# New states in 64x64 tiles over two PSUM banks, ahead of the values from the state, in an mLSTM with an MLP behind it

## The chip, the cores and the metric

One core of a Trainium2 chip runs the whole kernel. The metric is the time of one execution on the device, in microseconds (us); lower is better. All engines of the core (TensorE, VectorE, ScalarE, GpSimd, and SyncE, which issues most DMAs) work on the one program and wait for each other by semaphores.

## What is computed

An mLSTM over 4 batches, 8 heads, 768 steps of time and heads of width 40, followed by a gated MLP (320 to 2048 to 320) on all 3072 tokens, in float32:

```python
for t in range(S):
    m_new = np.maximum(f_gate[:, :, t] + m, i_gate[:, :, t])
    f_stab = np.exp(f_gate[:, :, t] + m - m_new)
    i_stab = np.exp(i_gate[:, :, t] - m_new)
    m = m_new
    C = f_stab[:, :, None, None] * C + i_stab[:, :, None, None] * np.einsum('bhd,bhe->bhde', vt, kt)
    n = f_stab[:, :, None] * n + i_stab[:, :, None] * kt
    h_tilde = np.einsum('bhde,bhe->bhd', C, qt)
    denom = np.maximum(np.abs(np.einsum('bhd,bhd->bh', n, qt)[:, :, None]), 1.0)
    y[:, :, t] = 1.0 / (1.0 + np.exp(-o_gate[:, :, t])) * h_tilde / denom
...
h = x @ w_in
return (h * (1.0 / (1.0 + np.exp(-h))) @ w_out).astype(np.float32)
```

## The kernel before, in words

Time is cut into 12 chunks of 64 steps, the batches into 2 pairs. A *unit* is one chunk of one pair: 64 steps x 2 batches x 8 heads; there are 24, numbered 0 to 23. Three units make a *step* of 384 tokens for the MLP (8 steps, `j`), and the MLP of a step walks over 16 blocks of 128 hidden features (`fc`).

For a unit, `scores` (L516) multiplies keys and queries of the chunk, `weigh` (L550, instruction at L551) multiplies the scores by the decay in place, `near_values` (L587, matmuls at L595) applies them to the values of the chunk, `far_values` (L604, L610) adds what comes from the state Cm of the chunks before, `norm`, `level` and `scale` (L619 to L655) divide by the denominator and apply the output gate, which gives x. `state` (L660) makes what the chunk adds to the state (pu, from the weighted keys kw and the values vt), and `carry` (L677) decays the state on GpSimd (L688) and adds pu to it on VectorE (L694), for the two halves `a` of the partitions in turn. Chunk 11 has no new state, so units 0 to 21 have one. Scores and near values run in 64x64 tiles of TensorE; far values and states use all rows (104 or 128) and 64 columns. The values are 41 wide, as a column of ones brings the denominator along.

From step 2 on, x is turned by a transposition on VectorE (`turn_out`, L701), four writes to DRAM (L703) and, two `fc` later, a read back (`turn_in`, L711), all on SyncE's queue; five `fc` after the block ScalarE and VectorE split it into a high and a low part (`xput`, L740 and L741). In steps 0 and 1 TensorE transposes x (L729).

The MLP of step j and the units of step j + 1 are woven together by hand: the schedule is manual, and the order of the program is the order on each engine. `mm1` (L761, matmuls at L784) makes ph for one `fc`, 8 matmuls from step 1 on; `act` (L788) makes the tanh on ScalarE (L791), then the gating on VectorE (L805, L797 in step 0), the high part on ScalarE (L810), the low part on VectorE (L814); `mm2` (L819, matmuls at L835) uses them two `fc` later. Three places in each step (PLACES, L41: `fc` 1, 5 and 9 from step 2 on) hold a unit's block. There TensorE gets, between `mm1` and `mm2`,

```python
        if n + 1 < NU:
            units[n + 1].scores(pair)
        u.place(pair)
        u.near_values()
        u.far_values()
        u.state()
```

so the scores of the next unit and the values of this one lie in one PSUM tile (`couple`, psP, one buffer). The weighting of unit n + 1 and the norm of unit n follow in `close` (L879), from within `act`, and level, scale, turn_out and carry behind it. ph lies in the pool psH, two banks used in turn; pu lies in psU, one bank. A tile can be written once every access to the tile that had its buffer before is done.

Of the kernel before, what the change touches and what calls it, by code (L numbers as in the profile page):

```python
# [8 lines left out]
F32 = mybir.dt.float32  # L9
# [5 lines left out]
ALU = mybir.AluOpType  # L15
# [3 lines left out]
B, H, S, D = 4, 8, 768, 40  # L19
L = 64  # L20
# [6 lines left out]
UPS = 3  # L27
# [3 lines left out]
D1 = D + 1  # L31
# [12 lines left out]
def mlstm_mlp_kernel(  # L44
# [12 lines left out]
    nc = tc.nc  # L57
# [7 lines left out]
    psH = pool("psH", 2, space=PSUM)  # L65
    psP = pool("psP", 1, space=PSUM)
    psU = pool("psU", 1, space=PSUM)
# [12 lines left out]
    for k in range(2):  # L80
        m = mask[k * L : (k + 1) * L]
        nc.gpsimd.affine_select(
            out=m, in_=m, compare_op=ALU.is_ge, fill=NEG, base=0,
# [264 lines left out]
    def bank(n, pool_, tag, shape, name):  # L348

        if n < UPS:  # L350
            return pool_.tile(shape, F32, tag=tag, name=name)
        return psU.tile(shape, F32, tag="u", name=name)

    def couple(name):

        return psP.tile([128, H, 128], F32, tag="p", name=name)

    class Unit:
# [301 lines left out]
        def state(self):  # L660
            n, c, p = self.n, self.c, self.p
            if c == NC - 1:
                return
            pu = bank(n, psO, "o", [128, H, D1], f"pu{n}")
            by_d = pu.rearrange("p (d j) f -> p j d f", d=2)
            for j in range(4):
                for a in range(2):
                    nc.tensor.matmul(  # L668
                        by_d[a * 64 : a * 64 + D, j],
                        self.kw[:, a * 4 + j, :],  # L670
                        self.vt[:, :, a * 4 + j, :],
                        start=True,
                        stop=True,
                    )
            self.pu = pu

        def carry(self, copy=nc.scalar.copy):  # L677
            n, c, p = self.n, self.c, self.p
            if c == NC - 1:
                return  # L680
            pu = self.pu
            for a in range(2):
                r = slice(a * 64, a * 64 + D)
                v = Cm[p][r, a, :].rearrange("p (h e) -> p h e", e=D1)
                if c == 0:
                    copy(v, pu[r])
                    continue
                nc.gpsimd.tensor_tensor(  # L688
                    out=v,
                    in0=v,  # L690
                    in1=self.lq[r, :, L - 1].unsqueeze(2).broadcast_to([D, H, D1]),
                    op=ALU.mult,
                )
                nc.vector.tensor_tensor(out=v, in0=v, in1=pu[r], op=ALU.add)  # L694

        def turn_out(self):

# [168 lines left out]
    def block(n):  # L866

        u = units[n]
        if n + 1 < EARLY and n + 2 < NU:
            units[n + 2].load()  # L870
        pair = couple(f"p{n + 1}")
        if n + 1 < NU:
            units[n + 1].scores(pair)
        u.place(pair)
        u.near_values()
        u.far_values()
        u.state()

    def close(n):  # L879
        if n + 1 < NU:  # L880
            units[n + 1].weigh()
        units[n].norm()

    def turn(n):
        if n + 1 >= EARLY and n + 3 < NU:
            units[n + 3].load()
        if n + 2 < NU:
            units[n + 2].load_q()
            units[n + 2].shift()
        if n % UPS == 0:  # L890
            steps[n // UPS] = Step(n // UPS)
        if n < 3 * UPS:
            units[n].xpose()
            units[n].xput(steps[n // UPS])
# [172 lines left out]
    for j in range(NSTEP):  # L1067
        st = steps[j]
        for fc in range(NFC):
            at = {}  # L1070
            if j < NSTEP - 1:
                at = {fc - a: units[(j + 1) * UPS + u] for u, a in enumerate(PLACES[min(j, 2)])}
            if j == 0 and fc in KEYS:
                units[KEYS[fc]].keys()
            st.mm1(fc)
            if 0 in at:
                block(at[0].n)
                st.act(fc, between=lambda: close(at[0].n))
                at[0].level()
                at[0].scale()  # L1080
                if j > 1:
                    at[0].turn_out()
                at[0].carry()
            else:
                st.act(fc, splits=[SPLITS[x[0]](int(x[1])) for x in LOWS.get((j, fc), ())])
            if 2 in at and at[2].n + 1 < NU:
                if at[2].n + 2 < NU:
                    units[at[2].n + 2].exp()
                units[at[2].n + 1].misc()
            if j > 0 and 3 in at and at[3].n + 2 < NU:  # L1090
                units[at[3].n + 2].keys()
            if fc >= LAG and (j, fc) != (NSTEP - 1, NFC - 1):
                st.mm2(fc - LAG)
            elif fc < LAG and j > 0:
                steps[j - 1].mm2(NFC - LAG + fc)
            if 1 in at:
                turn(at[1].n)
                if at[1].n + 2 < NU:
                    units[at[1].n + 2].add()
            if j > 1 and 5 in at:  # L1100
                at[5].xput(steps[j + 1])
            if j > 1 and 2 in at:
                at[2].turn_in()
            if j == 0:
                FILL[fc]()
# [78 lines left out]
```

## Time and profile before

| | us |
|---|---|
| median of 3 runs | 441.98 |
| lowest and highest | 441.46, 442.47 |
| the profiled execution's own time | 440.74 |
| its span, first to last instruction | 439.0 |
| TensorE busy | 433.2 (99%) |
| VectorE busy | 278.0 (63%) |
| ScalarE busy | 211.8 (48%) |
| GpSimd busy | 124.2 (28%) |

The granted clock of TensorE is full in all 40 slices of the profile. Names in the rows: PE is TensorE's matmuls, PEld its weight loads, which overlap them, DVE is VectorE, ACT ScalarE, POOL GpSimd, SP SyncE. L595 is line 595 of the kernel. `p<-vb,D` reads: tile p is written from vb and D. Where a row of the timeline merges instructions of one line, the second number is the time from the start of the first to the end of the last.

### The profile page before, as it was taken

How to read it: one execution, taken by the hardware profiler on the slowest of the kernel's cores; microseconds unless marked ns; L12 is line 12 of the kernel's file. 1: busy time of each engine (PE TensorE's matmuls, PEld its weight loads, DVE VectorE, ACT ScalarE, POOL GpSimd, SP SyncE). 2: the span in 40 equal slices, each digit the busy share in tenths (PEclk: the TensorE clock that was granted, in tenths of full speed). 3: DMA queues.
4: the chain of work that ended last, by engine and by line, in shares of the span. 5: the costliest groups of instructions: out<-in, count | busy, mean ns of one | idle time of the engine just before them, and what ended most of it. 6: DMA issues, size and time to landing. Idle time of an engine off the chain costs nothing.

```text
span 439.0 us, 11120 instructions
## 1 busy us (share of the span) xinstructions
PE 433.2 (99%) x4437; PEld 399.9 (91%) x4437; DVE 278.0 (63%) x610; ACT 211.8 (48%) x439; POOL 124.2 (28%) x135
## 2 busy tenths in 40 slices
PE   8999999999999999999999999999999999999996
PEld 4767667799999999999999999999999999999995
DVE  5798789577875577466664676455674655444442
ACT  7783955545744444444444533544344444443332
POOL 5834144133233243134230444122341311000000
PEclk9999999999999999999999999999999999999999
DMA  8999796251350565406751265603854131101001
GB/s 265 368 367 321 198 285 161 83 171 44 116 142 1 128 181 143 129 16 189 200 147 31 57 195 157 173 2 90 243 119 128 18 90 37 36 2 45 1 1 46
DMA packets 58644, 56.29 MB, mean 128 GB/s; under 512 B 28208, under 2 KB 45184, under 8 KB 58592
## 3 DMA queue, kind: packets, MB, share of 16 engines
q1 hardware_dynamic: 58288, 55.15, 44.0%
q8 instruction: 35, 0.57, 0.6%
q10 hardware_dynamic: 208, 0.26, 0.2%
q0 software_dynamic: 96, 0.16, 0.1%
q14 instruction: 17, 0.14, 0.1%
HBM read 48.59 MB, written 6.96 MB: 127 GB/s over the span
## 4 chain that ended last, share of the span: by engine, by line
PE 80%; issue 16%; DVE 1%; DMA 1%; ACT 1%; POOL 0%; POOLq 0%; DVEq 0%; ACTq 0%
PE ph L784 35%; PE pout L835 32%; PE p L524 3%; PE p L610 3%; PE pu L668 3%; PE p L595 2%; DMA home<-in_ig_dram 1%; PE p L729 0%; PE po L579 0%; PE px L729 0%; DVE D L551 0%; POOL qt L508 0%; PE pt L198 0%; PE ph L913 0%; PE e L384 0%
## 5 line engine op out<-in xcount | busy, mean ns | idle before, releaser
L791 ACT ACTIVATE th<-ph 128x384 f32<-128x384 f32 x128 | 62.5, 488 | 128.1 <-PE ph L784 127.6
L784 PE MATMUL ph<-xh,wh 128*128 128x384 f32 x336 | 113.9, 339 | 0.0
L784 PE MATMUL ph<-xl,wh 128*128 128x384 f32 x336 | 113.7, 338 | 0.0
L805 DVE SCALAR_TENSOR_TENSOR th<-th,ph 128x384 f32<-128x384 f32 x112 | 62.1, 555 | 74.2 <-ACT th L791 73.5
L835 PE MATMUL pout<-woh,gh 128*128 128x320 f32 x336 | 105.4, 314 | 0.0
L835 PE MATMUL pout<-woh,gl 128*128 128x320 f32 x336 | 103.9, 309 | 0.0
L835 PE MATMUL pout<-wol,gh 128*128 128x320 f32 x336 | 103.2, 307 | 0.0
L814 DVE TENSOR_TENSOR gl<-th,gh 128x384 fp32r<-128x384 f32 x112 | 65.5, 585 | 47.6 <-ACT gh L810 47.6
L810 ACT CAST gh<-th 128x384 fp32r<-128x384 f32 x112 | 57.5, 513 | 71.8 <-DVE th L805 71.2
L784 PE MATMUL ph<-xh,wl 128*128 128x384 f32 x224 | 76.0, 339 | 0.0
L835 PEld LDWEIGHTS pout<-woh,gh 128*128 128x128 f32 x336 | 63.0, 188 | 2.0
L784 PEld LDWEIGHTS ph<-xh,wh 128*128 128x128 f32 x336 | 63.1, 188 | 0.2
L835 PEld LDWEIGHTS pout<-woh,gl 128*128 128x128 f32 x336 | 63.0, 188 | 0.1
L784 PEld LDWEIGHTS ph<-xl,wh 128*128 128x128 f32 x336 | 63.0, 188 | 0.2
L835 PEld LDWEIGHTS pout<-wol,gh 128*128 128x128 f32 x336 | 63.1, 188 | 0.0
L688 POOL TENSOR_TENSOR Cm<-Cm,lq 40x328 f32<-40x328 f32 x40 | 30.5, 763 | 110.2 <-PE p L610 108.6
L508 POOL TENSOR_TENSOR qt<-qk,lq 104x512 f32<-104x512 f32 x22 | 28.7, 1306 | 115.6 <-ACT lq L504 103.0
L784 PEld LDWEIGHTS ph<-xh,wl 128*128 128x128 f32 x224 | 42.1, 188 | 0.0
L835 PE MATMUL pout<-wo,g 128*128 128x320 f32 x96 | 28.7, 435 | 0.0
L491 POOL TENSOR_TENSOR D<-D,am 128x512 f32<-128x512 f32 x20 | 26.2, 1310 | 5.9 <-DMA D<-LFd 3.9
L483 POOL TENSOR_TENSOR am<-mask,aT 128x512 f32<-128x512 f32 x20 | 24.1, 1206 | 6.6 <-DVE aT L205 5.1
L551 DVE TENSOR_TENSOR D<-p,D 128x512 f32<-128x512 f32 x24 | 16.5, 689 | 11.7 <-PE p L610 10.3
(126 smaller groups left out, 490.2 us busy)
## 6 DMA issues: line engine op xcount, KB each, us to landing
qk<-in_qk_dram SPq DMA_DIRECT2D x24, 512.0 KB, 4.9
ko<-in_ko_dram SPq DMA_DIRECT2D x24, 320.0 KB, 5.1
wro<-in_w_out_dram SPq DMA_DIRECT2D x8, 640.0 KB, 6.8
D<-LFd SPq DMA_DIRECT2D x40, 128.0 KB, 3.1
lq<-LFd SPq DMA_DIRECT2D x40, 128.0 KB, 4.5
wri<-in_w_in_dram SPq DMA_DIRECT2D x8, 512.0 KB, 5.8
vb<-in_vp_dram SPq DMA_DIRECT2D x48, 82.0 KB, 4.5
out_dram<-ob SPq DMA_DIRECT2D x45, 80.0 KB, 2.1
```

The costliest lines, as they stand in the source:

```text
L483: nc.gpsimd.tensor_tensor(out=self.am, in0=mask.unsqueeze(1).broadcast_to([128, H, L]), in1=aT[:, self.c, self.p, :].unsqueeze(2).broadcas ...
L491: nc.gpsimd.tensor_tensor(out=self.Dm, in0=self.Dm, in1=self.am, op=ALU.add)
L508: nc.gpsimd.tensor_tensor(out=self.qt, in0=self.q[:KS], in1=self.lq[:KS], op=ALU.mult)
L524: nc.tensor.matmul(self.ps[d * L : (d + 1) * L, a * 4 + j, :], self.k[r, d * 4 + j, :], self.q[r, d * 4 + j, :], start=True, stop=True,)
L551: nc.vector.tensor_tensor(out=self.Dm, in0=self.ps, in1=self.Dm, op=ALU.mult)
L688: nc.gpsimd.tensor_tensor(out=v, in0=v, in1=self.lq[r, :, L - 1].unsqueeze(2).broadcast_to([D, H, D1]), op=ALU.mult,)
L784: nc.tensor.matmul(ph, w, x, start=(i == 0), stop=(i == len(ops) - 1))
L791: nc.scalar.activation(th, ph, AF.Tanh, scale=0.5)
L805: nc.vector.scalar_tensor_tensor(out=th, in0=th, scalar=1.0, in1=ph, op0=ALU.add, op1=ALU.mult)
L810: nc.scalar.copy(gh, th)
L814: nc.vector.tensor_tensor(out=gl, in0=th, in1=gh.bitcast(F32), op=ALU.subtract)
L835: nc.tensor.matmul(self.po[t], g[:, ts], w, start=(fc == 0 and i == 0), stop=(last and i == len(ops) - 1),)
```

## The change

For units from the fourth on (`n >= UPS`, UPS is 3), the new state is made in 64x64 tiles: the two batches of the pair (d, which lie on the two halves of the partitions) are no longer one matmul over 128 rows and 82 columns (the other batch's values are zero in each half), but two over 64 rows and 41 columns. The part of d = 0 goes to a bank of psU, that of d = 1 to a bank of psH. The new state comes ahead of the far values. `carry` adds the parts one by one, four additions of 40x164 for two of 40x328, and it stands ahead of `turn_out`.

```diff
@@ state
+            if n >= UPS:
+                self.pu = [
+                    pool_.tile([128, 4, D1], F32, tag=tag, name=f"pu{n}_{tag}")
+                    for pool_, tag in ((psU, "u"), (psH, "h"))
+                ]
+                for j in range(4):
+                    for d in range(2):
+                        r = slice(d * L, (d + 1) * L)
+                        for a in range(2):
+                            nc.tensor.matmul(
+                                self.pu[d][a * 64 : a * 64 + D, j, :],
+                                self.kw[r, a * 4 + j, :],
+                                self.vt[r, d, a * 4 + j, :],
+                                start=True,
+                                stop=True,
+                            )
+                return
@@ carry
-                nc.vector.tensor_tensor(out=v, in0=v, in1=pu[r], op=ALU.add)
+                for d in range(2) if n >= UPS else ():
+                    w = v[:, d * 4 : (d + 1) * 4]
+                    nc.vector.tensor_tensor(out=w, in0=w, in1=pu[d][r], op=ALU.add)
+                if n < UPS:
+                    nc.vector.tensor_tensor(out=v, in0=v, in1=pu[r], op=ALU.add)
@@ block
         u.near_values()
+        u.state()
         u.far_values()
-        u.state()
@@ the loop over steps and fc
                 at[0].level()
                 at[0].scale()
+                at[0].carry()
                 if j > 1:
                     at[0].turn_out()
-                at[0].carry()
```

## Rows read from the trace of the kernel before

**Rows 1.** The page, busy us, share of the span and instructions of each engine.
```profile
PE 433.2 (99%) x4437; PEld 399.9 (91%) x4437; DVE 278.0 (63%) x610; ACT 211.8 (48%) x439; POOL 124.2 (28%) x135
```
**Rows 2.** Waits: who waited for whom: us in total, times, longest us.
```profile
DVE D L551 <- PE p L610: 10.3, 16, 0.7
...
ACT xh L740 <- DMA px<-xd: 2.9, 4, 1.3
```
**Rows 3.** Timeline of TensorE around unit 13: start, length in us, instructions.
```profile
203.08 0.63 PE L595 MATMUL p<-vb,D 64*64 64x41 f32 x32
203.64 0.79 PE L610 MATMUL p<-Cm,qt 104*64 104x82 f32 x16
204.25 0.74 PE L668 MATMUL pu<-vb,kw 128*40 128x82 f32 x16
204.92 0.42 PE L835 MATMUL pout<-woh,gh 128*128 128x320 f32 x1
205.18 0.31 PE L835 MATMUL pout<-wol,gh 128*128 128x320 f32 x1
205.32 0.31 PE L835 MATMUL pout<-woh,gl 128*128 128x320 f32 x1
...
206.34 0.34 PE L784 MATMUL ph<-xh,wh 128*128 128x384 f32 x1
...
209.05 0.34 PE L784 MATMUL ph<-xh,wh 128*128 128x384 f32 x1
```
**Rows 4.** Timeline of TensorE, windows that end at 203.19 and 203.25.
```profile
203.08 0.34 PE L595 MATMUL p<-vb,D 64*64 64x41 f32 x12
...
203.08 0.40 PE L595 MATMUL p<-vb,D 64*64 64x41 f32 x16
```
**Rows 5.** Single lines, weight loads and matmuls: ns min/median/max, first and last start.
```profile
L784 PEld LDWEIGHTS ph<-xh,wh x336: 186/188/190, 80.7 to 430.2; 128*128 128x128 f32 x168
...
L595 PEld LDWEIGHTS p<-vb,D x672: 129/135/135, 36.7 to 369.7; 64*64 64x64 f32 x168
...
L668 PEld LDWEIGHTS pu<-vb,kw x352: 112/115/118, 12.7 to 345.0; 128*40 128x40 f32 x176
L668 PE MATMUL pu<-vb,kw x352: 232/233/267, 12.7 to 345.1; 128*40 128x82 f32 x176
```
**Rows 6.** Timeline of VectorE around unit 13.
```profile
203.53 0.56 DVE L805 SCALAR_TENSOR_TENSOR th<-th,ph 128x384 f32<-128x384 f32 x1 [0.72 <-ACT th L791]
...
206.93 0.68 DVE L655 SCALAR_TENSOR_TENSOR x<-ko,p 128x256 f32<-128x256 f32 x3
207.65 0.58 DVE L701 STREAM_TRANSPOSE xt<-x 128x384 f32<-128x384 f32 x1
208.15 0.98 DVE L694 TENSOR_TENSOR Cm<-Cm,pu 40x328 f32<-40x328 f32 x2
```
**Rows 7.** VectorE's groups by shape: busy us, mean ns, idle us before.
```profile
L694 DVE TENSOR_TENSOR Cm<-Cm,pu 40x328 f32<-40x328 f32 x40 | 19.2, 479 | 0.7
L655 DVE SCALAR_TENSOR_TENSOR x<-ko,p 128x256 f32<-128x256 f32 x21 | 8.9, 422 | 0.7
...
L655 DVE SCALAR_TENSOR_TENSOR x<-ko,p 128x64 f32<-128x64 f32 x42 | 7.3, 214 | 0.0
```
**Rows 8.** Timeline, VectorE and weight loads, behind unit 3 in step 0.
```profile
46.62 0.69 DVE L257 SCALAR_TENSOR_TENSOR wi<-wri 128x512 uint32<-128x512 uint32 x1 [0.52 <-ACT wri L256]
...
47.36 0.62 PEld L784 LDWEIGHTS ph<-x,wi 128*128 128x128 f32 x3 [0.52 <-DVE wi L257]
```
**Rows 9.** Timeline of VectorE and TensorE behind unit 6, in step 1.
```profile
93.25 1.01 DVE L694 TENSOR_TENSOR Cm<-Cm,pu 40x328 f32<-40x328 f32 x2
...
95.04 0.43 PE L784 MATMUL ph<-xh,wh 128*128 128x384 f32 x1
```
**Rows 10.** Timeline, the turned x of unit 14 and the next step's first matmul.
```profile
235.30 0.56 DVE L741 TENSOR_TENSOR xl<-px,xh 128x384 fp32r<-128x384 f32 x1 [0.74 <-ACT xh L740]
...
236.13 0.34 PE L784 MATMUL ph<-xh,wh 128*128 128x384 f32 x1
```

## The prediction, made before the change had run

> **What bounds the kernel now.** I read the busy shares first. TensorE is busy 433.2 of 439.0 us [rows 1], and in the middle of the run nothing stops it, so time is gained only where TensorE's own stream gets shorter, and any new wait in that stream is paid in full. The view of waits, read second, names TensorE in no long wait; it shows two queues hanging on it that matter here. VectorE's weighting (L551) waits 16 times for the end of the far values (L610), although what it needs is the scores: scores and values share one PSUM tile. And ScalarE already waits four times for the turned x to come back from DRAM [rows 2].
>
> Third, the timeline of one block, unit 13 in step 3; the others from unit 9 on look alike within 0.03 us. The near values start at 203.08, the far ones at 203.64, the state at 204.25, and MLP work goes on at 204.92 [rows 3]. The first matmul of the next fc comes at 206.34 and that of the one after it at 209.05 [rows 3]. 19 units (3 to 21) have the changed state: three in step 0, three in step 1, thirteen later.
>
> **The state on TensorE.** Each fp32 matmul is two records. Today's state is 16 records in pairs; they last 0.74 with 0.233 for the last [rows 3, 5], so the eight pairs are 0.072 apart, 0.57 in all. The new one is 32 records in eight groups of four, in the tile form of the near values, with 41 moving columns and 40 weight columns for 64. What is a group worth? The near values give the upper end: between 12 and 16 records the stretch grows from 0.34 to 0.40 [rows 4], so 0.058 a group (0.06 as shown; 32 records fit in 0.56). The lower end is half of today's pair, since half the columns pass: 0.036. Which one holds depends on what sets the near values' pace. A weight load takes 188 ns for 128 columns, 135 for 64, 115 for 40 [rows 5]: 0.83 ns a column, 53 ns for 64, just under the 58, and 33 for 40. I read the 58 as the load's pace, and then 40 columns run at the matmul's own; I take 0.040, nearer the lower end. The state then pushes the far values back by 0.058 + 7 x 0.040 = 0.34 (0.31 to 0.46), and TensorE gains 0.57 - 0.34 = 0.23 a block (0.11 to 0.26). Leaving the 64x64 form costs a pause either way: it stands before the far values today and will stand there again. That MLP work follows the far values instead of the state I cost at nothing, as both fill all rows in 64 columns (bound: 0.1 either way).
>
> If all of that came through, 19 x 0.23 = 4.4 us would go. Two things stand against it.
>
> **The borrowed bank.** Half the state now takes a place in the ring of two banks that hold ph. The next ph (206.34) must therefore wait for this fc's L805, done at 204.09 [rows 3, 6]: a margin of 2 us, so nothing. But the ph after that (209.05) takes the bank in which the state lies, and waits until VectorE's last addition has read it. VectorE's chain runs from the far values' end without a gap: weighting, norm, gl, level, scale, ending at 206.93 + 0.68 = 207.61 [rows 6]. It moves with the far values, by 0.34. Then come four additions of 164 elements for two of 328. One of 328 takes 479 ns; L655 takes 422 ns for 256 elements and 214 for 64, or 1.08 ns an element [rows 7], so 164 take about 0.31. Three L655 in a row last 0.68 where their own times add up to 0.85: instructions on the same partitions overlap by 0.085. Today's two additions, on different partitions, last 0.98 [rows 6] and don't overlap. The new order is two on one partition range, then two on the other: 4 x 0.31 - 2 x 0.085 + 0.03 = 1.10 (0.98, as today, if half the length costs half; 1.33 if nothing overlaps). They may start 0.08 before the scale ends, as today's start at 208.15 before the transposition ends at 208.23 [rows 6]. So the bank is free at 207.61 - 0.08 + 0.34 + 1.10 = 208.97, and 0.05 later the weight load can start, as it did behind L257 (ends 47.31, load at 47.36) [rows 8]. A matmul behind a cold load loses another 0.11: 204.92 to 205.18 is 0.26, the next step 0.15 [rows 3]. That gives 209.13. Without the wait it would be 209.05 - 0.23 = 208.82. So the block gains 0.23 and then waits 0.31: **0.08 lost**, and 0.05 in the five first blocks of a step, which start 0.02 later: 8 x 0.08 + 5 x 0.05 = 0.89 us.
>
> In steps 0 and 1 the transposes of x lie in between and there is no turning through DRAM. In step 1 the additions start at 93.25 [rows 9]: 93.25 + 0.34 + 1.10 + 0.05 + 0.11 = 94.85 against 95.04 today; 0.19 gained, three times, 0.57. In step 0 there is more room, but after unit 3 TensorE waits 0.52 for a weight part anyway [rows 8], which eats that unit's share: 2 x 0.23 = 0.46.
>
> **The addition ahead of turn_out.** The transposition (L701, 207.65 [rows 6]) now starts behind the additions, at 209.00: 1.35 later. Behind it on SP's queue stand the four writes to DRAM, the output's stores in a step's first block, the next unit's loads, and the read of the turned x; they follow each other almost without gaps, so all move. The loads are issued some three blocks ahead and stay covered; the read is less so. Of the four waits for it [rows 2] one is a step's third unit, 14: its xl is done at 235.30 + 0.56 = 235.86, and the next step's first matmul is at 236.13 [rows 10]. With 1.35 more, that matmul waits about 1.1. The other three waits are of first units, whose late x delays only an activation. I take 0.5 (0 to 2). That L805 of the next fc stands behind additions and transposition (0.45 later) costs nothing: its bank is wanted 1.5 us later.
>
> **Sum.** 0.89 - 0.57 - 0.46 + 0.5 = +0.4 us. On the profiled execution (440.74 us, 439.0 span) that is 441.1; against the median of 441.98, 1.2 above it, **442.3 us**, no change. A measurement of this kernel tells some 0.2% (0.9 us) from nothing. This case by itself spans 441.0 to 444.0.
>
> **Rivals.**
> *The state runs at the near values' pace* (0.058). For it: it is the only four-tile row with 41 columns. Against it: the load's length per column. The far values then move 0.46 and the block gains only 0.11; the ph waits until 209.25: 8 x 0.20 + 5 x 0.17 = 2.45 lost, 0.2 and 0.2 gained in steps 1 and 0, 0.5 for x: 444.5. It decides from 0.05 a group on.
> The Trainium skill (TensorEngine Tiling (Array Packing), Instruction Overhead) gives each matmul some 60 cycles of overhead, so that one of 1 column takes as long as one of 60; by that rule the 41 columns set the near values' pace, not the weights, the state would get the same 0.058, and the time would be this rival's rather than the sum's. The weight rows of this case speak for the other reading, without excluding it.
> *The bank comes back later still*: the four additions don't overlap (1.33), or the four tiles take turns in twos, so that the change doesn't do what it says. Either adds 0.23 to each wait: 13 x 0.3 = 3.9, with 0.5 for x and little gained before: 446. For it: today's additions don't overlap. Against it: L655 does.
> *The bank comes back in time*: faster. It would need VectorE to be done 0.35 earlier, with shorter additions or a weighting that no longer waits for the far values; then each block keeps its 0.23 and the time goes down to 437.6, or to some 440 if half of the wait goes. For it: four terms of the chain are estimates of a tenth each. Against it: the 16 waits of L551.
>
> **Chances.** The forecast 0.42 (same 0.31, slower 0.09, faster 0.02); near values' pace 0.18, slower; later still 0.15, slower but for 0.02; in time 0.25, of it 0.02 within 0.2%. That makes faster 0.25, same 0.35, slower 0.40. The range leaves a tenth out on each side: 439.6 to 445.8.
>
> **What would show it.** The state's records in groups of four some 0.04 apart (0.058 for the rival) and the far values 0.34 behind today's place; a wait of ph (L784) for the additions to Cm, 13 times, some 0.3 each, two fc after each block from step 2 on, and none in step 0; the four additions within 1.1; ScalarE's wait for px grown by about 1.3 each. No wait of L784 for VectorE would make the prediction wrong on the fast side; waits of 0.5 on the slow side.

## The result, and the profile after

| us | before | after |
|---|---|---|
| median, same chip (6 runs each) | 441.49 | 444.70 |
| lowest and highest | 441.3, 442.47 | 443.2, 445.76 |
| the profiled execution's own time | 440.74 | 444.32 |
| its span | 439.0 | 442.5 |

The change makes the kernel slower, by 0.7%: ratio 1.0067 [1.0046, 1.0087], 3.2 us. The range (439.6 to 445.8) held the time, but the forecast, no change, did not come: 442.3 was 2.4 us too low. Of the change itself, +0.4 forecast, 2.8 were missing, as the kernel before is 0.5 faster here than the median that the prediction started from.

The page's first and fourth part, of the kernel after:
```profile
span 442.5 us, 11784 instructions
...
PE 432.1 (98%) x4741; PEld 395.3 (89%) x4741; DVE 282.2 (64%) x648; ACT 211.2 (48%) x439; POOL 123.1 (28%) x135
...
PE 60%; issue 18%; DVE 12%; DMA 5%; ACT 3%; SPq 2%; POOL 0%; POOLq 0%; DVEq 0%; ACTq 0%
```
TensorE is busy 1.1 us less than before [rows 1] in a span that is 3.5 longer: its stream did get shorter, and it now stands still at times. The last line is the chain of work that ended last, followed back from the end. Before, it ran through VectorE and DMAs for 1% each; now 12% and 5%. The view of waits says where:
```profile
DVE D L551 <- PE p L610: 13.8, 16, 1.0
ACT xh L761 <- DMA px<-xd: 7.1, 7, 1.9
...
PEld ph L805 <- PE pout L856: 5.0, 12, 0.4
...
PE ph L805 <- DVE Cm L713: 3.5, 13, 1.3
```
Each line gives us in total, times, and the longest. The last is new: ph (now L805) waits 13 times for the additions to Cm (L713). The line above it is the weight load of the same ph, which stands just ahead of the matmul and whose wait the profile puts down to pout; the two overlap, so their totals aren't added. ScalarE's wait for the turned x went from four times and 2.9 us [rows 2] to seven times and 7.1.

The timeline of TensorE around unit 13 (its near values start at 203.83, against 203.08 before):
```profile
203.83 0.63 PE L595 MATMUL p<-vb,D 64*64 64x41 f32 x32
204.27 0.21 PE L673 MATMUL pu_u<-vb,kw 64*40 64x41 f32 x1
...
204.31 0.20 PE L673 MATMUL pu_u<-vb,kw 64*40 64x41 f32 x1
...
204.55 0.20 PE L673 MATMUL pu_u<-vb,kw 64*40 64x41 f32 x1
...
204.70 0.79 PE L610 MATMUL p<-Cm,qt 104*64 104x82 f32 x16
205.41 0.42 PE L856 MATMUL pout<-woh,gh 128*128 128x320 f32 x1
...
206.83 0.34 PE L805 MATMUL ph<-xh,wh 128*128 128x384 f32 x1
...
209.89 0.41 PE L805 MATMUL ph<-xh,wh 128*128 128x384 f32 x1 [0.19 <-DVE Cm L713]
210.14 0.34 PE L805 MATMUL ph<-xl,wh 128*128 128x384 f32 x1
```
```profile
209.86 0.19 PEld L805 LDWEIGHTS ph<-xh,wh 128*128 128x128 f32 x1 [0.42 <-PE pout L856]
```
The first record of the first group of four tiles is at 204.27, of the second at 204.31, of the eighth at 204.55: 0.040 a group. The far values come 0.87 behind the near ones (0.56 before [rows 3]), the first mm2 1.58 (1.84 before), the next fc's ph 3.00 (3.26 before). So TensorE's stream is 0.26 shorter. The ph after that comes at 6.06 behind the near values, against 5.97 before [rows 3], and its second matmul is 0.25 later, not 0.17 as in a warm stream: the 0.26 is gone, and more.

VectorE's timeline of the same block, and the additions' groups by shape (busy us, mean ns, idle us before):
```profile
205.53 0.69 DVE L551 TENSOR_TENSOR D<-p,D 128x512 f32<-128x512 f32 x1 [0.70 <-PE p L610]
...
207.99 0.68 DVE L655 SCALAR_TENSOR_TENSOR x<-ko,p 128x256 f32<-128x256 f32 x3
208.59 0.31 DVE L713 TENSOR_TENSOR Cm<-Cm,pu_u 40x164 f32<-40x164 f32 x1
208.83 0.31 DVE L713 TENSOR_TENSOR Cm<-Cm,pu_h 40x164 f32<-40x164 f32 x1
209.17 0.33 DVE L713 TENSOR_TENSOR Cm<-Cm,pu_u 40x164 f32<-40x164 f32 x1
209.42 0.32 DVE L713 TENSOR_TENSOR Cm<-Cm,pu_h 40x164 f32<-40x164 f32 x1
209.77 0.58 DVE L722 STREAM_TRANSPOSE xt<-x 128x384 f32<-128x384 f32 x1
```
```profile
L713 DVE TENSOR_TENSOR Cm<-Cm,pu_u 40x164 f32<-40x164 f32 x38 | 12.1, 319 | 0.5
L713 DVE TENSOR_TENSOR Cm<-Cm,pu_h 40x164 f32<-40x164 f32 x38 | 12.0, 317 | 0.0
```
The scale ends 4.84 behind the near values (4.53 before), the four additions take 1.15, and the weight load starts 0.12 behind the last of them. The transposition starts at 5.94 behind the near values, 4.57 before [rows 6]: x is turned 1.37 later.

What that does is seen in the step of units 18 to 20. Timelines of SyncE's queue, ScalarE, VectorE and TensorE; unit 20's near values start at 321.07:
```profile
300.44 2.85 SPq L724 DMA_DIRECT2D xd<-xt  x4
303.38 3.70 SPq L881 DMA_DIRECT2D out_dram<-ob  x6
...
312.51 0.59 SPq L732 DMA_DIRECT2D px<-xd  x1
...
317.04 0.51 ACT L761 CAST xh<-px 128x384 fp32r<-128x384 f32 x1 [1.91 <-DMA px<-xd]
...
323.45 0.69 DVE L551 TENSOR_TENSOR D<-p,D 128x512 f32<-128x512 f32 x1
...
324.70 1.33 DVE L835 TENSOR_TENSOR gl<-th,gh 128x384 fp32r<-128x384 f32 x1
...
326.47 0.68 DVE L655 SCALAR_TENSOR_TENSOR x<-ko,p 128x256 f32<-128x256 f32 x3
...
328.35 0.41 PE L805 MATMUL ph<-xh,wh 128*128 128x384 f32 x1 [1.32 <-DVE Cm L713]
```
Unit 18's x is written from 300.44 on; its read stands on the queue behind six stores of the output and eight loads and is issued at 312.51. ScalarE waits 1.91 for it. TensorE needs that x only in the next step, but ScalarE and VectorE pass the MLP's activations to each other in order, and both are still late when unit 20's block comes: the weighting starts 2.38 behind the near values, not 1.70, with no wait for TensorE left; gl takes 1.33, not 0.76; the scale ends 6.08 behind, not 4.84. So about half of the 1.24 is the late start, and nearly half is the longer gl. The additions end as much later, and ph waits 1.32 instead of 0.19. The lesser waits for a first unit's x did no such harm: ScalarE waits 0.41, 0.38 and 0.99 for units 9, 12 and 15, and the third units' blocks two places on still end their scale 4.84 or 4.85 behind.

The distance from one block's near values to the next's sums this up (timelines of TensorE):

| kernel, profiled run | inside a step | across a step's end | disturbed ones |
|---|---|---|---|
| before | 13.45 | 24.35 | none |
| after | 13.60 | 24.5 | 24.65, 24.61, 25.72 |
| e10_ahead_alone | 13.43 | 24.34 | none |
| e1_borrowed_first | 13.19 | 24.1 | 14.86, 25.53, 25.69, 24.63, 14.64, 26.44 |
| e3_state_behind | 13.31 | 24.31 | 25.46, 13.63, 26.01, 14.14, 26.01 |
| e5_read_ahead | 13.60 | 24.50 | none over 0.12 |
| e6_first_and_read | 13.20 | 24.1 | none |

The profiled runs of e1 and e3 (446.47 and 446.83 us) are 2.3 and 3.6 above the medians of their kernels, and e3's is the longest of its ten: their rows show what a disturbed block looks like, not how much of it a usual run has.

From unit 9's near values to unit 22's, 13 blocks, the change loses 3.33 in the profiled runs (221.90 against 218.57); from unit 3's to unit 9's it gains 0.86 (100.68 against 101.54). The start up to unit 3 was 1.0 longer in this one execution, but lies between 36.8 and 39.4 in the others', both kernels' and the experiments', and isn't the change's.

### The profile page after: what moved, and what is told of

It is laid out like the page before. It is cut to its first block, busy times and chain, and to the rows that moved or that the text cites. A ratio compares the mean times of both kernels' runs of the same rounds, so it can differ in the third digit from the quotient of the medians.

```text
span 442.5 us, 11784 instructions
## 1 busy us (share of the span) xinstructions
PE 432.1 (98%) x4741; PEld 395.3 (89%) x4741; DVE 282.2 (64%) x648; ACT 211.2 (48%) x439; POOL 123.1 (28%) x135
## 4 chain that ended last, share of the span: by engine, by line
PE 60%; issue 18%; DVE 12%; DMA 5%; ACT 3%; SPq 2%; POOL 0%; POOLq 0%; DVEq 0%; ACTq 0%
PE ph L805 28%; PE pout L856 22%; PE p L610 3%; DVE Cm L713 3%; PE p L524 3%; DVE gl L835 2%; DVE D L551 2%; PE p L595 2%; DMA qk<-in_qk_dram 2%; DMA ko<-in_ko_dram 1%; DMA lq<-LFd 1%; DVE x L655 1%; DVE p L636 1%; DMA px<-xd 1%; PE pu_u L673 1%
## 5 line engine op out<-in xcount | busy, mean ns | idle before, releaser
L805 PE MATMUL ph<-xh,wh 128*128 128x384 f32 x336 | 114.8, 342 | 3.5 <-DVE Cm L713 3.5
L805 PE MATMUL ph<-xl,wh 128*128 128x384 f32 x336 | 113.7, 338 | 0.0
L835 DVE TENSOR_TENSOR gl<-th,gh 128x384 fp32r<-128x384 f32 x112 | 66.2, 591 | 47.6 <-ACT gh L831 47.6
L805 PE MATMUL ph<-xh,wl 128*128 128x384 f32 x224 | 75.9, 339 | 0.0
L805 PEld LDWEIGHTS ph<-xh,wh 128*128 128x128 f32 x336 | 63.1, 188 | 7.0 <-PE pout L856 5.0
L805 PEld LDWEIGHTS ph<-xl,wh 128*128 128x128 f32 x336 | 63.0, 188 | 0.5 <-DVE xl L762 0.2
L805 PEld LDWEIGHTS ph<-xh,wl 128*128 128x128 f32 x224 | 42.1, 188 | 0.0
L491 POOL TENSOR_TENSOR D<-D,am 128x512 f32<-128x512 f32 x20 | 25.9, 1296 | 7.1 <-DMA D<-LFd 4.3
L483 POOL TENSOR_TENSOR am<-mask,aT 128x512 f32<-128x512 f32 x20 | 23.9, 1195 | 6.6 <-DVE aT L205 5.1
```

The source lines that it names most:

```text
L483: nc.gpsimd.tensor_tensor(out=self.am, in0=mask.unsqueeze(1).broadcast_to([128, H, L]), in1=aT[:, self.c, self.p, :].unsqueeze(2).broadcas ...
L491: nc.gpsimd.tensor_tensor(out=self.Dm, in0=self.Dm, in1=self.am, op=ALU.add)
L805: nc.tensor.matmul(ph, w, x, start=(i == 0), stop=(i == len(ops) - 1))
L835: nc.vector.tensor_tensor(out=gl, in0=th, in1=gh.bitcast(F32), op=ALU.subtract)
```

## The experiments

All times are medians; each kernel's runs stand beside runs of the kernel before on the same chip (441.41 to 441.55 us there), and ratios are to those, with their 95% intervals.

**The bank alone, the order alone.** Theory at first: the loss is the 13 waits for the borrowed bank. Four kernels, each with one part of the change undone, or one part alone.

e1 adds the halves of the state that lie in ph's bank first, for both partition ranges:
```diff
-                for d in range(2) if n >= UPS else ():
-                    w = v[:, d * 4 : (d + 1) * 4]
-                    nc.vector.tensor_tensor(out=w, in0=w, in1=pu[d][r], op=ALU.add)
...
+            for d in (1, 0) if n >= UPS else ():
+                for a in range(2):
+                    r = slice(a * 64, a * 64 + D)
+                    w = Cm[p][r, a, d * 4 * D1 : (d + 1) * 4 * D1].rearrange("p (h e) -> p h e", e=D1)
+                    nc.vector.tensor_tensor(out=w, in0=w, in1=pu[d][r], op=ALU.add)
```


> VectorE's four additions stand in another order: the two that read the borrowed bank of psH first, then the two of psU; nothing else differs from the changed kernel. My theory (the time went into ph's wait for the borrowed bank, 13 times from step 2 on): the bank is free about 0.58 us earlier, the 13 waits of L805 for the additions go, each block keeps its 0.25 us, and the time falls from 444.7 to about 439 us (437.5 to 440.5); what x comes late costs stays. Rival (the late turning of x is what costs, the bank little): x is as late as before, so 444 us. Second rival (a VectorE chain that starts later costs by itself): 444 us too.

Measured: 444.16 us, 1.0056 [1.0032, 1.0079], runs from 442.02 to 447.15. The theory missed its time, but not its mechanism. Waits, and the timelines of ScalarE, VectorE and TensorE in unit 11's block (near values at 166.37):
```profile
ACT xh L763 <- DMA px<-xd: 14.4, 8, 3.2
...
PE ph L807 <- DVE Cm L717: 2.6, 3, 0.9
PE ph L807 <- DVE th L828: 2.6, 2, 1.4
```
```profile
162.61 0.51 ACT L763 CAST xh<-px 128x384 fp32r<-128x384 f32 x1 [3.21 <-DMA px<-xd]
...
170.27 1.34 DVE L837 TENSOR_TENSOR gl<-th,gh 128x384 fp32r<-128x384 f32 x1
...
173.46 0.41 PE L807 MATMUL ph<-xh,wh 128*128 128x384 f32 x1 [0.87 <-DVE Cm L717]
```
Ten of the 13 bank waits are gone and an undisturbed block takes 13.19, less than before. But the wait for x doubles to 14.4 us, and ph waits again, for the additions in third units' blocks or for the gating in second units'. In part that is the edit itself: each of its additions works on the other partition range than the one ahead of it, they take 1.38 together instead of 1.15, and x is turned 6.18 behind the near values instead of 5.94. In part TensorE, no longer held in each block, comes sooner to where x is needed, by 0.2 from the near values to the cast (20.98 in e6, 21.19 in the changed kernel). The rest of the growth was not followed. So there are two costs, and each hides the other.

e2 turns x first again and adds behind it:
```diff
-                at[0].carry()
                 if j > 1:
                     at[0].turn_out()
+                at[0].carry()
```


> The changed kernel with turn_out ahead of the additions again. Theory: x is turned some 1.1 us earlier, but the bank comes back 0.50 us later in 13 blocks: 6.5 us lost, about 1.5 us regained from x, 449.7 us (448 to 451). Rival (late x is what costs): back to 441 or 442 us.

Measured: 450.05 us, 1.0181 [1.0157, 1.0206]. Waits:
```profile
PEld ph L805 <- PE pout L856: 13.0, 13, 1.0
PE ph L805 <- DVE Cm L713: 10.0, 13, 0.8
...
ACT xh L761 <- DMA px<-xd: 1.4, 1, 1.4
```
x is on time but for once, and ph waits 0.8 for the bank in each of 13 blocks. Given this bank, additions ahead of turn_out are the better order of the two by more than 5 us (450.05 against 444.70).

e3 puts the new state behind the far values:
```diff
         u.near_values()
-        u.state()
         u.far_values()
+        u.state()
```


> The changed kernel with the state behind the far values again, in 64x64 tiles and two banks. Theory: the far values and so VectorE's chain are 0.31 us earlier, the bank is back in time and the 13 waits go; TensorE pays one more pause between tile forms, so that a block gains only about 0.1 us instead of 0.25: 440.5 us (439.5 to 441.5). Rival (late x): x is still about a microsecond late, 443.5 to 444.5 us.

Measured: 443.20 us (443.02 without its longest run), 1.0033 [1.0009, 1.0056]. The theory's 440.5 missed. An undisturbed block takes 13.31, 0.14 less than before: VectorE's chain starts earlier than in the changed kernel, so that the bank is back in time. Yet ScalarE waits 10.5 us for x, and five blocks are disturbed. That profile is of the longest run, 446.83, so the size says little; that late x holds the median too is shown by e9 below, which has x on time and is some 3.7 faster.

e4 is the kernel before with its two long additions ahead of turn_out:
```diff
                 at[0].scale()
+                at[0].carry()
                 if j > 1:
                     at[0].turn_out()
-                at[0].carry()
```


> The kernel before with nothing but carry ahead of turn_out (two additions of 328 elements, one bank, state behind the far values). It has the late x alone, by 1.0 us. Theory: at most a microsecond, 441.5 to 442.5 us. Rival (late x is what costs): 443.5 to 445 us.

Measured: 442.85 us, 1.0029 [1.0013, 1.0044], between the two. Here no bank is borrowed, so its 1.4 us is not the bank's: ScalarE waits for x 10.0 us in all, and of the distances between blocks two have grown, to 24.79 and, past unit 20's block, 25.60, from 24.35.

**The read of x.** Theory now: late x costs some 2 us beside the bank's waits and much more once they are gone. The read is issued one fc earlier and ahead of the next unit's loads instead of behind them (e5 on the change, e7 on the kernel before, e6 on e1, e9 on e3); the split into high and low part goes just ahead of it, since its place in the ring is used again:
```diff
+            if j > 1 and 5 in at:
+                at[5].xput(steps[j + 1])
             if 1 in at:
+                if j > 1:
+                    at[1].turn_in()
                 turn(at[1].n)
...
-            if j > 1 and 5 in at:
-                at[5].xput(steps[j + 1])
-            if j > 1 and 2 in at:
-                at[2].turn_in()
```


> The changed kernel with the read of the turned x (turn_in) one fc earlier, ahead of the next units' loads on SyncE's queue, and the split of x (xput) just ahead of it; the bank is given back as in the changed kernel. Theory, as the first four runs leave it: two costs, ph's 13 waits for the borrowed bank and the late x, whose wait on ScalarE is carried over into the block behind the next. This takes the late x away and leaves the bank: the waits for px go to nearly nothing, the 13 waits of ph stay, 441.8 to 443 us. Rival (the bank is the whole cost, the late x only looks bad): no change from 444.5 us. Rival (late x is the whole cost): 438.5 to 440 us.

Measured: 442.53 us, 1.0031 [1.0010, 1.0052]. No wait for px is left, and every block still takes 13.60. So late x cost the change 444.70 - 442.53 = 2.2 us by the medians, and the bank keeps the rest: from unit 9 to 22 this profiled run is 1.95 longer than that of the kernel before, 0.15 a block. By the profiled runs alone late x is 3.33 - 1.95 = 1.4 (the changed kernel's runs differ by 2.6 among themselves).

> The kernel before with the read of the turned x ahead of the loads, as a control for e5 and e6. Theory: TensorE waits for nothing there, so 441.0 to 441.6 us. Rival (the early read is a gain by itself): 439 to 440 us.

Measured: 441.45 us, 0.9996 [0.9978, 1.0015]. In the kernel before, the early read is worth nothing: the four waits for x cost nothing there.

> Both remedies: the borrowed bank is read first, as in e1, and the read of the turned x goes ahead of the loads, as in e5. Theory: nothing stands against TensorE's gain of 0.25 us in each of 13 blocks and about 0.9 us in steps 0 and 1: 437.3 us (436.5 to 438.5), faster than both kernels. Rival (there is a third cost, such as VectorE's longer chain or loads that come late): 440 us or more.

Measured: **437.59 us, 0.9909 [0.9879, 0.9940]**, faster than both kernels. The page, and timelines of VectorE, SyncE, TensorE and ScalarE around unit 13 (near values at 202.49):
```profile
span 436.3 us, 11785 instructions
...
PE 428.6 (98%) x4741; PEld 395.6 (91%) x4741; DVE 281.5 (65%) x648; ACT 210.1 (48%) x439; POOL 123.1 (28%) x135
```
```profile
207.25 0.67 DVE L717 TENSOR_TENSOR Cm<-Cm,pu_h 40x164 f32<-40x164 f32 x2
207.95 0.68 DVE L717 TENSOR_TENSOR Cm<-Cm,pu_u 40x164 f32<-40x164 f32 x2
208.66 0.58 DVE L724 STREAM_TRANSPOSE xt<-x 128x384 f32<-128x384 f32 x1
...
208.05 0.19 PEld L807 LDWEIGHTS ph<-xh,wh 128*128 128x128 f32 x1
208.19 0.34 PE L807 MATMUL ph<-xh,wh 128*128 128x384 f32 x1
...
209.27 1.87 SPq L726 DMA_DIRECT2D xd<-xt  x4
212.58 0.38 SPq L734 DMA_DIRECT2D px<-xd  x1
213.06 2.00 SPq L430 DMA_DIRECT2D D<-LFd  x2
...
223.47 0.51 ACT L763 CAST xh<-px 128x384 fp32r<-128x384 f32 x1
```
The additions from ph's bank end at 207.92, 0.27 ahead of ph at 208.19, which waits for nothing. But ph's weight load stands at 208.05, only 0.13 behind them, and in the changed kernel it started 0.12 behind: there is nothing to spare. The read of x goes ahead of the loads, and the cast of it doesn't wait. The four medians side by side:

| | x late | x on time |
|---|---|---|
| bank waits | 444.70 | 442.53 |
| bank in time | 444.16 | **437.59** |

The bank's cure alone brings 0.5, which the intervals don't tell from nothing, that of x alone 2.2, both together 7.1. The first row's step of 2.2 is 6.6 in the second: with the bank in time, late x costs three times as much (x being another 0.24 later there).

**Three more.** e8 splits the additions: from step 2 on the decay and the additions from ph's bank go ahead of level and scale, those from psU behind the transposition, so that both resources come earlier; the loop's part of the edit:
```diff
...
+                if j > 1:
+                    at[0].carry(later=True)
                 at[0].level()
                 at[0].scale()
-                at[0].carry()
                 if j > 1:
                     at[0].turn_out()
+                    at[0].gather(0)
+                else:
+                    at[0].carry()
```


> The changed kernel from step 2 on with the decay and the two additions of the borrowed bank ahead of level and scale, and the two additions of psU behind turn_out. The bank comes back over a microsecond earlier; x is turned about 1.0 us later than before instead of 1.5. Theory: no wait for the bank, some late x left, about as in e4: 439.5 us (438.5 to 441). Rival (bank alone): 437.5 us. Rival (late x as bad as in e1): 443.5 us.

Measured: 439.74 us, 0.9950 [0.9927, 0.9973]. Blocks take 13.20, as in e6, though the additions from ph's bank are done 1.1 us earlier than there: so e6 loses nothing to the bank. But without the early read ScalarE still waits for x 7.7 us in seven waits, and e6 stays 2.1 ahead.

> e3 (state in 64x64 tiles behind the far values, four additions ahead of turn_out) with the early read of x of e5. It tells the tiles from their place. Theory: e3's missing gain was the late x; the bank is back in time, TensorE keeps about 0.12 us in each of 19 blocks, 439.3 us (438.5 to 440.3). Rival (the tiles bring their gain in either place): 437.5 us. Rival (nothing is left of it there): 441.5 us.

Measured: 439.46 us, 0.9960 [0.9936, 0.9985]: with x on time the new state is worth having behind the far values too. As long as the additions take the two banks in turn, the change's own place for it, ahead of them (e5), is 3.1 worse; with the borrowed bank read first (e6) it is 1.9 better, 13.20 a block for 13.31.

e10 is the kernel before with its old state (two long groups) ahead of the far values:
```diff
         u.near_values()
-        u.far_values()
         u.state()
+        u.far_values()
```


> The kernel before with nothing but the old state (one bank, 128 rows) ahead of the far values. VectorE's chain then starts 0.57 us later, with no borrowed bank to give back and x late by 0.57 us only. Theory: 441.4 to 442.5 us. Rival (a later VectorE chain costs by itself): 443 us or more.

Measured: 441.19 us, 0.9997 [0.9970, 1.0025]. That VectorE's chain starts later (the weighting of unit 13 starts 1.94 behind the near values instead of 1.39) costs nothing as long as no bank that ph needs hangs on its end.

## Why the prediction was right or wrong

**The state on TensorE: right.** 0.040 a group was taken and 0.040 measured; the far values moved back 0.31 (0.34 predicted), and 0.26 a block was gained (0.23). The rival of the near values' pace (0.058) fell: 41 columns behind 40 weight columns go faster than 41 behind 64. The Trainium skill (TensorEngine Tiling (Array Packing), Instruction Overhead) gives a matmul of 1 column the latency of one of 60, by some 60 cycles of overhead; taken as a pace, as that rival took it, it would have made the two alike, and these rows do not agree. That weights set the pace is what the prediction read from the loads' lengths. It went by the near values as the only four-tile row with 41 columns and left out the scores, which are a four-tile row too, with 64 moving columns and 64 weight columns (timeline of TensorE in the kernel after, windows that end at 203.65 and 203.70):
```profile
203.31 0.52 PE L524 MATMUL p<-qk 40*64 40x64 f32 x20
203.31 0.58 PE L524 MATMUL p<-qk 40*64 40x64 f32 x24
```
They too take 0.06 a group as shown, like the near values. So 64 or 41 moving columns behind 64 weight columns go at one pace, and 41 behind 40 go faster: in these three rows the pace goes with the weight columns. All of it comes out in e6: 3.9 us against the 4.4 named for the case in which nothing stands against it.

**The borrowed bank: mechanism right, size short.** 13 waits of ph for the additions came, from step 2 on, as the prediction said. It put the loss at 0.08 a block, 0.89 in all; e5, where nothing else is left, shows 0.15 and 1.95. ph's weight load was predicted at 209.02 - 203.08 = 5.94 behind the near values and came at 209.86 - 203.83 = 6.03: the far values' move was 0.03 less, the additions took 1.15 for 1.10, and the load came 0.12 behind the last addition where 0.05 was read from L257 [rows 8]. The cold start cost 0.03 from load to matmul and 0.25 - 0.17 = 0.08 behind it, the 0.11 of the prediction. So 0.09 was missing, and it doubles a loss that was the small rest of 0.23 gained and 0.31 waited. Most of it, 0.07, is the way from VectorE to the load, and the trace shows why L257 was no measure for that. Semaphore instructions of TensorE's queue at ph's line, before and after (count, ns):
```profile
L784 PEldq EVENT_SEMAPHORE  x7: 51/51/51, 19.1 to 385.7; - x7
...
L805 PEldq EVENT_SEMAPHORE  x26: 51/51/51, 20.3 to 389.2; - x26
```
There are 19 more, one for each unit with the new state. In each of the 13 blocks one stands between the last addition and the load: it starts 0.04 behind the addition's end, and the load 0.08 behind its start. Behind L257 none stands, and the load itself takes the wait.

**The additions' overlap: right in kind.** Two on one partition range start 0.24 apart; where the range changes, 0.34, so the third waits for the end of the second. The Trainium skill (VectorE: DVE Perf Modes, Two Vector instructions with no wait between them) says that an instruction whose inputs or output start in another quadrant of partitions than the last ones did is held until all earlier ones have finished; these rows agree, and so do e6's, where each addition changes the range and they start 0.33 or more apart.

**Steps 0 and 1: nearly right**, 0.86 gained for 1.03. Step 1's three blocks gain 0.19, 0.19 and 0.16 for the 0.19 predicted of each, so step 0 was the one that gained less than thought.

**Late x: the step that failed.** Transposition and writes did move by 1.37 (1.35 predicted), and the reads were issued 1.2 to 2.5 later (units 9 to 19, behind their near values). But the sum took 0.5 for it, on the words "The other three waits are of first units, whose late x delays only an activation". It measured 2.2 by the medians (e5), 1.4 in the profiled runs. It is a first unit that hurts most: its read stands behind the output's six stores as well, and an activation that waits long enough on ScalarE holds all that is behind it on ScalarE and, by the gating, on VectorE, whose chain in the third unit's block frees TensorE's bank. In the profiled run one wait of four was long enough, unit 18's 1.91, and it made the way past unit 20's block 25.72 instead of 24.51. The two terms were costed one by one; they meet in one chain. The wait that it did expect, 1.1 of the next step's first matmul for the third unit's x, came to little: the way from unit 14's block to unit 15's is 24.65 here and 24.50 with the early read. There the read was issued 2.4 later than before, but its x came only 0.6 later (the cast starts 18.81 behind the near values, 18.23 before), so that most of the delay was lost on the way.

By measured terms: 1.95 - 0.86 + 2.2 = 3.3 us, against 3.2; with the profiled runs' 1.4 for late x it is 2.5. The prediction had 0.89 - 1.03 + 0.5 = 0.4. So the bank is 1.1 of what was missing, late x 0.9 to 1.7, and steps 0 and 1 are 0.2.

**The rivals.** "The bank comes back in time" was given 437.6 in the prediction; e6 takes it there by the order of the additions, with 437.59, but only because x is on time; e1, the bank without the read, is 444.16. That the figures meet so closely is luck: the prediction took 4.4 from 441.98, and e6 gains 3.9 on 441.50. "The near values' pace" had been priced at 444.5, close to the 444.70 measured, and that is luck too, for its pace did not come. "Later still" didn't come: two additions on one range overlap, and the four tiles run at once. Nor did any case of the prediction have x cost more than 2, or the two costs hide each other; that the range held the time owes as much to its width as to its terms.

**Left open.** Whether both halves of the state could lie in one bank was not tried. How many blocks late x disturbs differs between executions: e1's runs spread over 5 us; which transfers collide in a given run wasn't followed.

## What to carry to other kernels

A stall that removes work's slack elsewhere can hide a second one: if curing one brings nothing, look in the waits for the queue that has grown longer, and cure both before the idea is given up. A tile borrowed from a ring is free when its last reader is done, so read the borrowed half first, whatever the order of the loops, and look at what that order costs the next in line (here x came 0.24 later). A wait on ScalarE for something that is needed much later isn't free where ScalarE and VectorE take turns in program order; put a read back ahead of the loads that have blocks of time.

## What the runs showed of the hardware beyond that

The same gl (128x384, L835) takes 0.56 as a rule, 0.76 in a unit's block and 1.33 in the disturbed one, where it starts 0.13 behind GpSimd's mask product (L483, 324.57, 1.04 long), with GpSimd's next product (L491) beside the rest of it. From unit 9 on the kernels after, e1, e3, e4 and e8 have eleven such gl between them, each 1.32 to 1.34 long and 0.12 or 0.13 behind the mask product; e5, e6, e7 and e9, which have x on time, have none. This was seen, not tried by itself. A weight load behind VectorE's last addition starts 0.12 after its end, with a semaphore instruction between the two, and behind L257, with none, 0.05 [rows 8].
